# The subtractions and normalisations of the last two pairs of heads may also run on VectorE, and the order of the attention is searched anew

## The chip, the cores and the metric

The kernel runs on one core of a Trainium2 chip. The metric is device time in microseconds (us), from one launch. The kernel before was timed three times.

## What is computed

Attention over 8 batches of 8 heads (576 tokens, 64 channels), in which every score more than tau below its row's maximum is dropped, and behind it a mixture of 8 experts in which each token goes to at most one expert. Cut to what matters:

```
scores = scale * q @ k^T
keep   = scores >= max(scores) - tau
attn   = softmax over the kept scores
x      = attn @ v                                # 4608 tokens x 512
active = x @ w_skip > 0
e      = argmax(x @ w_gate);  g = its softmax weight
out    = x + active * g * (relu(x @ w1[e]) @ w2[e])
```

## The kernel before

**Tiles.** A pair of heads of one batch is one unit g; there are 32 (NG), four to a batch. Keys lie on the partitions. For each head there are four tiles of 128 keys, and a ninth tile holds the 64 remaining keys of both heads. For each pair and tile, TensorE computes scores (L797), ScalarE takes the exponential (`e`, L967), and VectorE keeps or zeroes it (`p`, L972, in float32). Two tiles of p (128 x 1152; the ninth, 128 x 576, alone) are then split in two halves of 16 bits: ScalarE or VectorE rounds p to `ph` (`fph`, by L540 or L542), and `fpl` subtracts: pl = p - ph (L1009). In `fpl` the engine is written out: `nc.gpsimd`. The product with v needs three products for each block (ph with v's high half, ph with v's low half, pl with v's high half: L1037, L1040, L1041). Before all that, the maximum of each row comes from a second computation of the scores (L824, with the maximum on VectorE at L829), and its threshold is brought into row form by transposes (L919, L923).

**Normalisation.** When both heads of a pair are done, ScalarE copies the sums out (`a`), `fz` and `fr` make the reciprocal `z`, and two multiplications write the output of the pair: `fx` (L1091, 128 x 512, tile xb) and `ft` (L1104, the 64 remaining tokens, tile x2). Both are written out as `nc.gpsimd`.

**The way to the experts.** From x come transposes (L1147), the logits (L1173, and L1234 for the remaining tokens), the gate on VectorE (L1271 to L1367), scatters of token numbers (L1395, issued on GpSimd), lists (L1638, SyncE), and gathers of rows of x for each expert (L529). The expert with most tokens is begun early: after the gate of batch 6 its number is picked, its weights are loaded and split (`wh0` on ScalarE; `wl0`, L1541, on VectorE or GpSimd), 256 of its tokens are gathered (xg0), transposed (L1570) and sent through its first layer (L1603): eight groups of 12 matmuls, which the order may put anywhere from there on. Its second layer (L1891) and the other experts follow in an order written out by hand. In it VectorE splits the second layer's weights (L1818), clears two tiles (L2029) and only then turns the lists into numbers for the next gather (L1823).

**What sets the order.** The attention's operations, up to the early first layer, are not issued in the order of the code. Each is handed to a planner (`Plan`) with a key, the operations it depends on, and a table of engines with a length for each; `place` (L210) runs forward in its own time and always takes the ready operation with the smallest rank, on the engine that is free first. An operation that names two engines is placed on either. The rank of the first pass is the key; each of the 41 numbers in SEEDS then gives a new pass, with the ranks of the pass before it shifted a little, by a number drawn from the seed. The order of the last pass is what is built. Each engine runs its own instructions strictly in that order, and waits on semaphores. Where the plan leaves TensorE without work, `emit` (L144) puts matmuls that compute nothing (`fill`, L548) in front of the next operation.

**VectorE and GpSimd.** An operation whose `port` names VectorE or GpSimd takes part in a rule of the plan: a GpSimd operation is put behind the last such VectorE operation, in the plan and with a wait in the program. p's buffers number four (PFB) and come free when `fpl` has read them; the three buffers for ph and pl (PHB) come free when TensorE has multiplied them.

Of the kernel before, what the change touches and what calls it, by code (L numbers as in the profile page):

```python
# [18 lines left out]
ALU = mybir.AluOpType  # L19
# [39 lines left out]
SHB = 2  # L59
QB = 3  # L60
EB = 2
PFB = 4
PHB = 3
HV = 4
# [25 lines left out]
)  # L90
DLAT = 0.7
OFF = dict(
    ld=-1282.9330312000948, hl=-1781.2292006134314, hlD=1248.8496803122823, loD=731.1664150661729, di=1177.335263688824, S=-1115.0015130209733, mx=-878.5280584804156, th=-441.38012807859695, tr=-924.0085545558162, tc=279.9815207656505, T=302.18323320365494, e=-632.0289199987741, p=-886.6770366002503, ph=412.4007253243831, phD=-839.1953621827544, pl=-866.5752770646977, av=358.6214955194119, ldv=-939.7929525171812, v=565.9412181202888, v0=372.25762442909286, fmA=151.44, ld0=-6.12908597837135, init=1546.1710225456764, row=-1865.5677081481308, dh=2611.857870733773, bd=-530.9955588485915, rsp=-121.81377175859078, vsp=205.19014870229796, L1=1064.7837013439314, sc=226.4129098429862,
)
# [277 lines left out]
def attn_moe_kernel(ctx: ExitStack, tc: tile.TileContext, qk, vl, tau, wg, w1, w2, out):  # L372
    nc = tc.nc
# [138 lines left out]
    NG = B * HP  # L512
    END = STEP * NG

    pl = Plan(tc)
    PE, DVE, ACT, POOL, SPQ = "PE", "DVE", "ACT", "POOL", "SP"
    BOTH = (DVE, POOL)
# [10 lines left out]
    def gather(dst, idx, n):  # L528
        return nc.gpsimd.indirect_dma_start(  # L529
            dst,  # L530
            None,
            out[0:n, :],
            bass.IndirectOffsetOnAxis(ap=idx, axis=0),
            bounds_check=n - 1,
            oob_is_err=False,
        )

    def copy(e, dst, src):
        if e == ACT:
# [4 lines left out]
    ring = pl  # L544
# [6 lines left out]
    T = {}  # L551
# [391 lines left out]
    def plan_weights(g, i):  # L943
        b, hp = divmod(g, HP)
        QK, BD = QKs[(g + 1) % QB], BDs[g % 2]
        n = STEP * g + i
        tail = i == NM
        h, kt = (2, 0) if tail else divmod(i if i < NM else i - 1, NM)
        z = ("p", g, h, kt // 2)
# [15 lines left out]
        def expo():  # L965
            T["e", g, i] = e = ap_.tile([P, 2, HS], F32, name="e", tag="e", bufs=EB)
            nc.scalar.activation(e, T["W", g, i][:, :, 0:HS], AF.Exp, bias=ntau, scale=0.125)  # L967
# [14 lines left out]
        s = pl.op(n + OFF["T"], score, deps + ring.take("sps", SPB), {PE: 1.14 if tail else 0.57})  # L982
        e = pl.op(n + OFF["e"], expo, [s] + ring.take("e", EB), {ACT: 0.66})
        m = pl.op(n + OFF["p"], mask, [s, e] + (ring.take("p", PFB) if kt % 2 == 0 else T["ms", g]), {DVE: 0.73})
        ring.free("sps", [m])
# [13 lines left out]
        nk = len(ms)  # L999
        name, bufs = ("tp", 2) if tail else ("ph", PHB)  # L1000
        w = nk * S
# [2 lines left out]
            T["ph", g, i] = ap_.tile([P, nk, S], F16, name=name + "h", tag=name + "h", bufs=bufs)  # L1004
            copy(e, T["ph", g, i], T[z][:, 0:nk])

        def fpl():
            T["pl", g, i] = ap_.tile([P, nk, S], F16, name=name + "l", tag=name + "l", bufs=bufs)
            nc.gpsimd.tensor_tensor(T["pl", g, i], T.pop(z)[:, 0:nk], T["ph", g, i], op=ALU.subtract)  # L1009

        ph = pl.op(
            n + OFF["ph"], fph, ms + ring.take(name, bufs), {ACT: w / 1200 + 0.093, DVE: w / 1920 + 0.06}, off={DVE: OFF["phD"]}, port=BOTH
        )
        lo = pl.op(n + OFF["pl"], fpl, [ph], {POOL: w * 0.00208 + 0.04})
        ring.free("p", [lo])
        T["P", g, i] = [ph, lo]
        if tail:
# [4 lines left out]
    def plan_av(g, h, parts, n):  # L1022
        b, hp = divmod(g, HP)
        hd = 2 * hp + h
        k = n + OFF["av"]
# [59 lines left out]
        zz = pl.op(k + 1, fz, [x, T["a0"]] + ring.take("z", 4), {ACT: 0.3})  # L1085
        zz = pl.op(k + 1.2, fr, [zz], {DVE: 0.11})

        def fx():
            if hp == 0:
                T["x", b] = ap_.tile([P, NM, DM], F32, name="xb", tag="xb")  # L1090
            nc.gpsimd.tensor_tensor(  # L1091
                T["x", b].rearrange("p c (h d) -> p h c d", d=D)[:, 2 * hp : 2 * hp + 2],
                T["a", g][:, :, 0:NM, 0:D],
                T["z", g][:, :, 0:NM].rearrange("p h (c o) -> p h c o", o=1).broadcast_to([P, 2, NM, D]),
                op=ALU.mult,
            )

        r0 = b % 2 * TL

        def ft():  # L1100
            if hp == 0 and b % 2 == 0:
                T["x2"] = ap_.tile([P, DM], F32, name="x2", tag="x2", bufs=1)
            rs = slice(r0, r0 + TL)
            nc.gpsimd.tensor_tensor(  # L1104
                T["x2"].rearrange("p (h d) -> p h d", d=D)[rs, 2 * hp : 2 * hp + 2],
                T["a", g][rs, :, NM, 0:D],
                T["z", g][rs, :, NM].rearrange("p (h o) -> p h o", o=1).broadcast_to([TL, 2, D]),
                op=ALU.mult,
            )

        x1 = pl.op(k + 1.5, fx, [zz] + (ring.take("xb", 2) if hp == 0 else T["xm", b, hp - 1]), {POOL: 1.1})
        xt = pl.op(
            k + 1.6, ft, [zz, x1] + (ring.take("x2", 1) if hp == 0 and b % 2 == 0 else T["xtm"][-1:]), {POOL: 0.31}
        )
        ring.free("a", [x1, xt])
        ring.free("z", [x1, xt])
# [4 lines left out]
        if hp == HP - 1 and b % 2 == 1:  # L1121
            xtm = list(T["xtm"])
# [1063 lines left out]
```

## Time and profile before

| | |
|---|---|
| device time, 3 runs | 901.28 us median (900.65 to 909.02) |
| the profiled execution, its own time | 895.38 us |
| its span | 893.5 us |
| TensorE matmul busy | 859.5 us, 96% |
| VectorE busy | 682.8 us, 76% |
| GpSimd busy | 666.6 us, 75% |
| ScalarE busy | 607.5 us, 68% |

Times in the profile's rows are microseconds from the start of the span, and lengths in microseconds, unless ns is written. PE is TensorE, DVE VectorE, ACT ScalarE, POOL GpSimd, SP SyncE (it issues most transfers). In a timeline, "[0.35 <-POOL phl L1009]" says that the engine stood idle for 0.35 us before this instruction, and that its wait was ended by GpSimd's instruction of line 1009 on tile phl. The attention ends with the last logits at 631.7 us; the experts fill the rest.

### The profile page before, as it was taken

The page shows a single profiled execution, that of the slowest core. Times are in us where ns is not written, and L with a number is a line of the kernel's source. Part 1 is how long each engine was busy: PE and PEld are TensorE (multiplying, and loading weights), DVE is VectorE, ACT ScalarE, POOL GpSimd, SP SyncE. Part 2 cuts the span into 40 slices and gives each one's busy share as a digit, 9 for nine tenths or more (in the row PEclk, how much of TensorE's full clock was granted, in tenths as well). Part 3 has the DMA queues.
Part 4 walks back from the last instruction along what each step waited for, and adds up shares of the span by engine and source line. Part 5 has one row for each costly group of instructions (what it writes and reads, how often), then busy time and mean ns, then how long its engine had stood idle before and what let it go on. Part 6 is the DMA issues. An engine that isn't in the chain of part 4 may idle for free. (4 is left out here: it accounts for less than half of the span.)

```text
span 893.5 us, 24884 instructions
## 1 busy us (share of the span) xinstructions
PE 859.5 (96%) x9745; PEld 802.5 (90%) x9745; DVE 682.8 (76%) x1605; ACT 607.5 (68%) x923; POOL 666.6 (75%) x461
## 2 busy tenths in 40 slices
PE   9999999999999999999999999989989999999997
PEld 6888999999999999998889998978879898999986
DVE  6888888988997878999888899894535554476782
ACT  1768988798988798888789878786314452454451
POOL 5576998799789798999899979999336455473463
PEclk9999999999999999999999999999999999999999
DMA  7996778569577767857865864523156635544540
GB/s 174 250 217 164 179 168 235 145 157 254 136 154 203 186 149 200 210 130 188 187 145 136 238 150 97 141 99 120 60 164 232 212 97 184 189 146 162 189 139 19
DMA packets 77422, 147.58 MB, mean 165 GB/s; under 512 B 28178, under 2 KB 28178, under 8 KB 77304
## 3 DMA queue, kind: packets, MB, share of 16 engines
q1 hardware_dynamic: 72616, 136.33, 57.9%
q0 software_dynamic: 4544, 9.65, 3.2%
q8 instruction: 77, 1.26, 0.6%
q14 instruction: 41, 0.34, 0.1%
q10 hardware_dynamic: 144, 0.00, 0.0%
HBM read 68.68 MB, written 15.21 MB: 94 GB/s over the span
## 5 line engine op out<-in xcount | busy, mean ns | idle before, releaser
L1009 POOL TENSOR_TENSOR phl<-p,phh 128x1152 f16<-128x1152 f32 x128 | 305.3, 2394 | 36.3 <-ACT phh L540 14.4
L829 DVE TENSOR_REDUCE mx<-banks 128x1 f32<-128x288 f32 x558 | 230.4, 448 | 27.6 <-PE banks L824 25.4
L972 DVE SCALAR_TENSOR_TENSOR p<-banks,e 128x576 f32<-128x576 f32 x288 | 214.3, 752 | 42.4 <-ACT e L967 38.2
L967 ACT ACTIVATE e<-banks,ntau 128x576 f32<-128x576 f32 x288 | 207.8, 739 | 49.8 <-PE banks L797 37.9
L824 PE MATMUL banks<-QK 128*128 128x288 f32 x1024 | 192.2, 306 | 6.5 <-DMA QK<-hl 4.1
L797 PE MATMUL banks<-QK 128*128 128x288 f32 x1024 | 183.6, 307 | 4.7 <-DVE p L972 2.9
L824 PEld LDWEIGHTS banks<-QK 128*128 128x128 f32 x1024 | 148.8, 188 | 11.5 <-DVE p L972 4.2
L797 PEld LDWEIGHTS banks<-QK 128*128 128x128 f32 x1024 | 145.9, 190 | 10.8 <-DVE p L972 6.3
L540 ACT ACTIVATE phh<-p 128x1152 f16<-128x1152 f32 x117 | 136.1, 1165 | 17.4 <-DVE p L972 10.8
L1037 PE MATMUL banks<-Vh,phh 128*128 128x65 f16 x1280 | 131.0, 195 | 0.4 <-ACT xf L540 0.4
L1041 PE MATMUL banks<-Vh,phl 128*128 128x65 f16 x1280 | 129.1, 194 | 1.1 <-POOL phl L1009 0.9
L1040 PE MATMUL banks<-Vl,phh 128*128 128x64 f16 x1280 | 129.9, 193 | 0.0
L1037 PEld LDWEIGHTS <-phh 128*128 128x128 f16 x1280 | 116.5, 98 | 7.1
L1041 PEld LDWEIGHTS <-phl 128*128 128x128 f16 x1280 | 117.3, 97 | 1.8 <-POOL phl L1009 1.7
L1040 PEld LDWEIGHTS <-phh 128*128 128x128 f16 x1280 | 117.5, 99 | 0.5 <-issue 0.4
L1818 POOL TENSOR_TENSOR wl<-wr,wh 128x1024 fp32r<-128x1024 f32 x28 | 72.5, 2606 | 33.5 <-ACT wh L1817 25.7
L1857 PE MATMUL hps<-xh,wl 128*128 128x256 f32 (+4 forms) x256 | 76.7, 300 | 0.0
L599 POOL TENSOR_TENSOR hl<-raw,hl 128x576 fp32r<-128x576 f32 x43 | 61.6, 1439 | 20.0 <-DVE hl L599 13.0
L1857 PE MATMUL hps<-xh,wh 128*128 128x256 f32 (+4 forms) x248 | 75.9, 306 | 0.0
L1857 PE MATMUL hps<-xl,wh 128*128 128x256 f32 (+4 forms) x248 | 74.8, 302 | 0.0
L1869 POOL DMA_INDIRECT out<-o,ids x21 | 21.1, 1004 | 71.9 <-DVE o L1868 29.2
L1858 ACT ACTIVATE QK<-hps 128x256 fp32r<-128x256 f32 (+4 forms) x64 | 26.9, 421 | 67.8 <-PE hps L1857 67.1
(251 smaller groups left out, 1882.1 us busy)
## 6 DMA issues: line engine op xcount, KB each, us to landing
QK<-hl SPq DMA_DIRECT2D x192, 288.0 KB
wr<-in_w SPq DMA_DIRECT2D x31, 1024.0 KB
raw<-in_qk SPq DMA_DIRECT2D x32, 576.0 KB
vraw<-in_vl SPq DMA_DIRECT2D x32, 320.0 KB
out<-xb SPq DMA_DIRECT2D x32, 256.0 KB
BD<-hl SPq DMA_DIRECT2D x64, 64.0 KB
QK<-QK SPq DMA_DIRECT2D x32, 76.5 KB
out<-x SPq DMA_DIRECT2D x8, 128.0 KB
```

Of the source, the lines that this page charges most:

```text
L540: nc.scalar.activation(dst, src, AF.Copy)
L797: nc.tensor.matmul(ps[:, j, 0:HS], w_, x_[:, js], start=(i == 0), stop=(i == len(mm) - 1))
L824: nc.tensor.matmul(ps[:, 0:HS], w_, x_[:, js], start=(q == 0), stop=(q == len(mm) - 1))
L829: nc.vector.tensor_reduce(T["mx", g][:, o, j : j + 1], T.pop(("S", g, i, j))[:, 0:HS], AX.X, ALU.max)
L967: nc.scalar.activation(e, T["W", g, i][:, :, 0:HS], AF.Exp, bias=ntau, scale=0.125)
L972: nc.vector.scalar_tensor_tensor(T[z][:, kt % 2].rearrange("p (a b) -> p a b", a=2), T.pop(("W", g, i))[:, :, 0:HS], 0.0, T.pop(("e", g, i ...
L1009: nc.gpsimd.tensor_tensor(T["pl", g, i], T.pop(z)[:, 0:nk], T["ph", g, i], op=ALU.subtract)
L1037: nc.tensor.matmul(pv[:, c, :], x, Vh[:, vh, kt, :], start=(j + q + c == 0), stop=False, skip_group_check=True)
L1040: nc.tensor.matmul(pv[:, c, 0:D], x, Vl[:, vh, kt, :], start=False, stop=False, skip_group_check=True)
L1041: nc.tensor.matmul(pv[:, c, :], y, Vh[:, vh, kt, :], start=False, stop=(c == NM), skip_group_check=True)
L1818: lo[q % 2].tensor_tensor(w[1][:, sl], rs, w[0][:, sl].bitcast(F32), op=ALU.subtract)
L1857: nc.tensor.matmul(hp_[:, 0:cap], w_, x, start=(i == 0), stop=(i == len(mm) - 1))
```

## The change

For the last two pairs (g = 30 and 31: `LASTS = 2`), `fpl`, `fx` and `ft` name both engines in their tables, with a length for VectorE beside that for GpSimd; for the other 30 pairs the table is as it was. 24 seeds are added behind the 41. Nothing that is computed changes, and no buffer. Line numbers of the code that follows are 9 higher in the changed kernel.

```diff
+LASTS = 2
 SEEDS = (
...
-    1038489, 1039139, 1039626, 1043379, 1053365,
+    1038489, 1039139, 1039626, 1043379, 1053365, 7000007, 7000031, 7000032, 7000052, 7000074, 7000122, 7000131,
...
+    def either(e):
+        return nc.gpsimd if e == POOL else nc.vector
+
+    def shared(g, pool, dve):
+        return {POOL: pool, DVE: dve} if g >= NG - LASTS else {POOL: pool}
...
-        def fpl():
+        def fpl(e):
             T["pl", g, i] = ap_.tile([P, nk, S], F16, name=name + "l", tag=name + "l", bufs=bufs)
-            nc.gpsimd.tensor_tensor(T["pl", g, i], T.pop(z)[:, 0:nk], T["ph", g, i], op=ALU.subtract)
+            either(e).tensor_tensor(T["pl", g, i], T.pop(z)[:, 0:nk], T["ph", g, i], op=ALU.subtract)
...
-        lo = pl.op(n + OFF["pl"], fpl, [ph], {POOL: w * 0.00208 + 0.04})
+        lo = pl.op(n + OFF["pl"], fpl, [ph], shared(g, w * 0.00208 + 0.04, w / 960 + 0.1), port=BOTH)
...
-        def fx():
+        def fx(e):
...
-            nc.gpsimd.tensor_tensor(
+            either(e).tensor_tensor(
...
-        def ft():
+        def ft(e):
...
-            nc.gpsimd.tensor_tensor(
+            either(e).tensor_tensor(
...
-        x1 = pl.op(k + 1.5, fx, [zz] + (ring.take("xb", 2) if hp == 0 else T["xm", b, hp - 1]), {POOL: 1.1})
+        x1 = pl.op(k + 1.5, fx, [zz] + (ring.take("xb", 2) if hp == 0 else T["xm", b, hp - 1]), shared(g, 1.1, 0.65), port=BOTH)
         xt = pl.op(
-            k + 1.6, ft, [zz, x1] + (ring.take("x2", 1) if hp == 0 and b % 2 == 0 else T["xtm"][-1:]), {POOL: 0.31}
+            k + 1.6, ft, [zz, x1] + (ring.take("x2", 1) if hp == 0 and b % 2 == 0 else T["xtm"][-1:]), shared(g, 0.31, 0.25), port=BOTH
         )
```

Because each pass starts from the one before, the new tables change the order from the first microseconds on: on every engine the first difference is among the first 15 planned operations. VectorE gets six of the ten subtractions of the two pairs (pair 30: three of its four wide ones; pair 31: three of its four wide ones), and both pairs' fx and ft.

GpSimd at the end of the attention, before, from the last scatters for batch 6 to the last subtraction (numbers tell tiles apart; phl and tpl are pl of a wide and of a ninth tile):

```order
L1395 DMA lst_68<-rec_11134,si_11136 36864x2 x3
L1009 TENSOR_TENSOR tpl_11728<-p_11561,tph_11598 128x576
L1009 TENSOR_TENSOR phl_11745<-p_11609,phh_11706 128x1152
L1009 TENSOR_TENSOR phl_11781<-p_11726,phh_11765 128x1152
L529 DMA xg0_11841<-out_0,id0_149 128x512 x2
L1009 TENSOR_TENSOR phl_11903<-p_11763,phh_11822 128x1152
L1009 TENSOR_TENSOR tpl_11930<-p_11901,tph_11912 128x576
L1009 TENSOR_TENSOR phl_11966<-p_11820,phh_11920 128x1152
L1009 TENSOR_TENSOR phl_11985<-p_11914,phh_11971 128x1152
L1009 TENSOR_TENSOR phl_12063<-p_11969,phh_12029 128x1152
L1091 TENSOR_TENSOR xb_11429<-a_11418,z_11730 128x2x4x64
```

The same place after the change, from the last scatters for batch 6 to the scatters for the last gate:

```order
L1404 DMA lst_68<-rec_11235,si_11237 36864x2 x4
L1100 TENSOR_TENSOR xb_11283<-a_11445,z_11616 128x2x4x64
L1018 TENSOR_TENSOR tpl_11936<-p_11903,tph_11919 128x576
L1113 TENSOR_TENSOR x2_10074<-a_11445,z_11616 64x128
L1018 TENSOR_TENSOR phl_12001<-p_11934,phh_11977 128x1152
L532 DMA xg0_12016<-out_0,id0_149 128x512 x2
L1550 TENSOR_TENSOR wl0_12091<-wr_11829,wh0_11932 128x512
L1404 DMA lst_68<-rec_12227,si_12229 36864x2 x5
```

Eight subtractions stood behind these scatters, and now two; the gather xg0 stood before the last five subtractions, and now stands behind the last.

VectorE around the last p of pair 31, after the change (id0 are the numbers for the gather xg0, wl0 the early weights' low halves; before, only p's, two reciprocals, id0 and wl0 stood there):

```order
L981 SCALAR_TENSOR_TENSOR p_11999<-banks_104,e_11970 128x576
L1507 CAST id0_149<-rec0_148 128x2
L1508 TENSOR_SCALAR id0_149<-rec0_148 128x2
L981 SCALAR_TENSOR_TENSOR p_11999<-banks_104,e_11995 128x576
L1196 TENSOR_TENSOR lg_10977<-lg_10977,banks_104 128x64
L1100 TENSOR_TENSOR xb_11283<-a_11757,z_11853 128x2x4x64
L1018 TENSOR_TENSOR phl_12064<-p_11999,phh_12013 128x1152
L1550 TENSOR_TENSOR wl0_12091<-wr_11829,wh0_11932 128x512
L1550 TENSOR_TENSOR wl0_12125<-raw2_11851,wh0_11932 128x512 x2
L1550 TENSOR_TENSOR wl0_12091<-wr_11829,wh0_11932 128x512
L1092 RECIPROCAL z_12136<-z_12136 128x10
```

The last subtraction and the normalisation of pair 30 have come into VectorE's queue, and four of the wl0 subtractions stand between that subtraction and the last reciprocal.

TensorE around the last logits, before: the third of the early first layer's groups of 12 ends here, and three such groups stand ahead of the last logits (L1234, L1173) and five behind:

```order
L1603 MATMUL banks<-QK_105,wl_11714 128x256
L1147 MATMUL banks<-ident,xb 128x128 x4
L1173 MATMUL banks<-wgt,xf 128x16 x6
L1147 MATMUL banks<-ident,x_10097 128x128 x4
L1173 MATMUL banks<-wgt,xf 128x16 x2
L1147 MATMUL banks<-ident,xb 128x128 x4
L1234 MATMUL banks<-wgt,xf 128x16 x4
L1173 MATMUL banks<-wgt,xf 128x16 x4
L1603 MATMUL banks<-QK_105,wh_11532 128x256
```

The same place after the change (L557 is `fill`, L1579 the transposes of the gathered tokens):

```order
L1579 MATMUL banks<-ident,xg_12016 128x128 x8
L557 LDWEIGHTS jt
L557 MATMUL banks<-jt 128x256
...
L1156 MATMUL banks<-ident,x_10074 128x128 x4
L1156 MATMUL banks<-ident,xb 128x128 x4
...
L1243 MATMUL banks<-wgt,xf 128x16 x4
L1182 MATMUL banks<-wgt,xf 128x16 x4
L1612 MATMUL banks<-QK_105,wh_11932 128x256
```

All eight groups of 12 now stand behind the last logits. Of the matmuls that compute nothing, 27 stood in the attention's last part before, and now 30; in its first 40 us there were 87, and now there are 95.

## Rows read from the trace of the kernel before

**Rows 1.** Busy time by stretch: engine, busy time, instruction count, then clock, transfers.

```profile
75.00:575.00 500.00, 486.93 (x6741) 464.47 (x6738) 433.90 (x1117) 422.60 (x631) 445.19 (x280) 1.00 0.70 173
...
575.00:600.00 25.00, 23.61 (x329) 21.12 (x328) 23.82 (x64) 21.10 (x32) 23.52 (x16) 1.00 0.26 94
600.00:625.00 25.00, 21.90 (x341) 20.27 (x340) 13.81 (x23) 16.42 (x26) 23.57 (x16) 0.93 0.31 110
```

**Rows 2.** Groups by line: GpSimd's wide subtraction; busy, mean ns, idle before.

```profile
L1009 POOL TENSOR_TENSOR phl<-p,phh 128x1152 f16<-128x1152 f32 x128 | 305.3, 2394 | 36.3 <-ACT phh L540 14.4
```

**Rows 3.** Timeline of GpSimd at the end of the attention: start, length, instruction.

```profile
614.72 7.04 POOL L1009 TENSOR_TENSOR phl<-p,phh 128x1152 f16<-128x1152 f32 x3
...
625.92 1.05 POOL L1091 TENSOR_TENSOR xb<-a,z 128x512 f32<-128x512 f32 x1 [1.08 <-DVE z L1083]
```

**Rows 4.** Timeline of TensorE, 595 to 617 us: its longer waits.

```profile
597.75 0.20 PE L1041 MATMUL banks<-Vh,phl 128*128 128x65 f16 x1 [0.35 <-POOL phl L1009]
...
599.37 0.78 PE L797 MATMUL banks<-QK 128*128 128x288 f32 x4 [0.59 <-ACT QK L929]
...
601.99 0.79 PE L797 MATMUL banks<-QK 128*128 128x288 f32 x4 [1.16 <-DVE p L972]
...
603.57 0.20 PE L1041 MATMUL banks<-Vh,tpl 128*128 128x65 f16 x1 [0.71 <-POOL tpl L1009]
...
615.85 0.99 PE L1570 MATMUL banks<-ident,xg 128*128 128x128 f32 x7 [1.10 <-DMA xg<-out,id]
```

**Rows 5.** Timeline of TensorE: matmuls that compute nothing, and eight score matmuls twice.

```profile
600.00 0.83 PE L548 MATMUL banks<-jt 128*128 128x256 f16 x6
...
604.23 2.27 PE L797 MATMUL banks<-QK 128*128 128x288 f32 x8
...
611.22 1.30 PE L797 MATMUL banks<-QK 128*128 128x288 f32 x8
```

**Rows 6.** Early first layer (L1603) by stretch: matmul busy, weight loads, granted clock.

```profile
631.50:637.20 5.70, 5.66 (x36) 5.62 (x37) 0.75 0.04 12
637.30:640.30 3.00, 2.98 (x25) 2.78 (x24) 1.00 0.00 0
```

**Rows 7.** Timeline of TensorE: last scores, last product, last logits, next expert's transposes.

```profile
612.50 0.77 PE L797 MATMUL banks<-QK 128*128 128x288 f32 x4
...
623.52 0.20 PE L1037 MATMUL banks<-Vh,phh 128*128 128x65 f16 x1
...
624.45 0.63 PE L1147 MATMUL banks<-ident,xb 128*128 128x128 f32 x4
...
630.37 1.33 PE L1173 MATMUL banks<-wgt,xf 128*128 128x16 f32 x8
...
655.17 1.45 PE L1839 MATMUL xtp<-ident,xg 128*128 128x128 f32 x4 [2.85 <-DMA xg<-out,ids]
```

**Rows 8.** Timeline of VectorE: last p, and its queue ahead of the next gather.

```profile
616.18 0.76 DVE L972 SCALAR_TENSOR_TENSOR p<-banks,e 128x576 f32<-128x576 f32 x1 [1.22 <-ACT e L967]
...
641.89 4.63 DVE L1818 TENSOR_TENSOR wl<-wr,wh 128x1024 fp32r<-128x1024 f32 x4 [0.25 <-ACT wh L1817]
...
648.40 1.34 DVE L2029 MEMSET xg<- 128x1536 f32 x1 [0.27 <-issue]
650.45 0.17 DVE L1823 CAST ids<-recs 128x2 int32<-128x2 f32 x1 [0.71 <-DMA recs<-lst]
```

**Rows 9.** Subtractions on VectorE by line: shortest, median, longest ns, starts, shape.

```profile
L1541 DVE TENSOR_TENSOR wl<-wr,wh x4: 678/678/2090, 596.2 to 599.4; 128x512 fp32r<-128x512 f32 x4
...
L1818 DVE TENSOR_TENSOR wl<-wr,wh x32: 1202/1225/7786, 641.9 to 874.0; 128x1024 fp32r<-128x1024 f32 x32
```

**Rows 10.** Timeline of GpSimd: the subtraction that ran at 596 us.

```profile
595.31 2.39 POOL L1009 TENSOR_TENSOR phl<-p,phh 128x1152 f16<-128x1152 f32 x1
```

**Rows 11.** Timelines: ScalarE's last ph, and GpSimd's second early gather.

```profile
617.70 1.16 ACT L540 ACTIVATE phh<-p 128x1152 f16<-128x1152 f32 x1
...
610.09 1.01 POOL L529 DMA_INDIRECT xg<-out,id  x1 [0.31 <-PE banks L797]
```

2 rows, old and new, of the table SEEDS are left out of this document.

## The prediction

> **What bounds the kernel now.** I read the busy times by stretch first, then the timelines of GpSimd, TensorE and VectorE at the end of the attention, then the durations by line. Between 75 and 575 us TensorE is busy 486.93 of 500 us, and nothing else comes near it [rows 1]: what counts there is TensorE's own 13.1 us of idle time. The picture changes behind 575 us. GpSimd is busy 23.52 and 23.57 of 25 us in the next two stretches, while TensorE falls to 21.90 in the second and its mean granted clock to 0.93 [rows 1]. The reader should see a backlog: GpSimd is still at three wide subtractions from 614.72 to 621.76 [rows 3], although the last p of the attention was done at 616.94 [rows 8], and the last product with v starts only at 623.52 [rows 7].
>
> What TensorE loses here can be summed up to 640.3 us, where the early first layer ends [rows 6]. Waits: 0.35 + 0.59 + 1.16 + 0.71 + 1.10 = 3.9 us [rows 4]. The 27 matmuls that compute nothing: six take 0.83 us, 0.14 each [rows 5], so 3.7 us. Slow clock: the eight score matmuls at 604.23 take 2.27 us, the same eight at 611.22 only 1.30 [rows 5], 1.0 us lost; and behind the logits 36 matmuls take 5.66 us at a granted clock of 0.75, where 25 take 2.98 at 1.00 (0.119 each, so 36 would take 4.3) [rows 6], 1.4 us; a mean of 0.75 is a mix of the clock's two levels, 1.2 and 2.4 GHz, and what TensorE did just before were the logits' small matmuls. Together 10.0 us, 1.1% of the time. That is all that the last part could give if TensorE's work stays as it is.
>
> Behind 640.3 another chain takes over. VectorE splits weights (4.63 us from 641.89), clears two tiles (the second ends at 649.74) and makes the numbers for the next expert's gather at 650.45, after 0.71 us of waiting for the lists [rows 8]; TensorE waits 2.85 us for that gather until 655.17 [rows 7]. So two things nearly tie there: the last logits (631.70 [rows 7]) plus 23.5 us, by gate, scatters and lists, and the end of the early first layer plus 14.9 us, by VectorE's queue; without the 0.71 us, 14.2.
>
> **The change, step by step.** *Off GpSimd:* six wide subtractions of 2.394 us [rows 2], 14.4 us, and two pairs' normalisations, 1.05 us for each fx [rows 3]. *Onto VectorE:* the same subtraction has not run there. Two inputs in SBUF of 512 columns take 0.678 us, of 1024 columns 1.202 to 1.225 [rows 9]; the slope gives 1.34 us for 1152. The upper bound is 1.34 plus a whole GpSimd subtraction, 3.73 us, if it stands behind one; I take 1.34, since in the new order GpSimd has only two subtractions left behind the scatters. Six make 8.0 us. fx lies between 0.68 (same width, rows 9) and GpSimd's 1.05; I take 0.68. ft is smaller and bounded by it. VectorE had 11.2 us idle between 600 and 625 [rows 1], so this fits, but not with much room.
>
> *Up to the last scores.* Before, the last score matmul ends at 613.27 [rows 7]. The waits before it are the first four, 2.8 us, with 16 of the 27 empty matmuls (2.2) and the slow 1.0: 6.0 us that the backlog costs there. In the new order 6 empty matmuls stand before it (0.8), and I leave 2.0 us of waits, since VectorE is now nearly full; the ends are 0 and 4 (as much as all five waits of rows 4). But 60 product matmuls and a group of transposes now come ahead of it, which stood behind: 30 products take the 0.93 us from 623.52 to the next transposes, and those 0.63 [rows 7], so 2.5 us. So the last scores end at 613.3 - 6.0 + 0.8 + 2.0 + 2.5 = 612.6.
>
> *From the last scores to the last logits.* Before, 18.4 us: 3.7 to the end of the last p [rows 7, 8], 4.8 until GpSimd's last subtraction, 1.8 until TensorE, busy with a group of the early layer, turns to the product, 8.2 to the end of the logits, another group of 12 among them (1.4 at 0.119). After: 3.7, then 1.16 for ph [rows 11] and 1.34 for pl, then 8.2 - 1.4 = 6.8 for the rest. I add 1.0: the gather xg0 now stands behind GpSimd's last subtraction, its transposes stand ahead of the last transposes of x in TensorE's queue, and its second half took 5.8 us from issue to use [rows 4, 11]. Sum 14.0, so the last logits end at 626.6, 5.1 us earlier.
>
> *And behind them* this is taken back in part. Three groups of the early first layer have left the space before the logits, and all eight now follow: 96 matmuls at 0.119 [rows 6] are 11.4 us, and the early layer ends at 638.0 instead of 640.3, only 2.3 earlier. VectorE's queue then needs its 14.2 us, so the next expert's transposes start at 652.2; by the logits alone they could start at 650.1. Before, 655.17: **3.0 us gained**, not 5.1. The second half of the weights for the second layer is now loaded behind the output rows, but stays covered by those 11.4 us. *First microseconds:* eight more empty matmuls, 0.14 each, **1.1 us lost**. *Between 75 and 575 us* the order is new everywhere; the 13.1 us of idle may be less or more. Bounds: 0 (a stretch like the best) and twice as much, 26 us, as the 575 to 600 stretch lost 1.39 in 25 us [rows 1], a rate of 28 in 500. I take no change.
>
> Sum: -3.0 + 1.1 = -1.9 us. The profiled execution's own time of 895.38 (its span and 1.9 us around it) would become 893.5; it lies 5.9 us under the median of the three runs, 901.28, and from that median the sum gives **899.4 us**.
>
> **The port.** Where VectorE subtracts while GpSimd is inside a subtraction, the two do not share: GpSimd's ran from 595.31 to 597.70 at its usual 2.39 [rows 10], while the first of VectorE's four, begun at 596.2, is the one of 2.09 instead of 0.678 [rows 9], which is about the wait to 597.70 and 0.6 more. The Trainium skill, page "SBUF — State Buffer", section "Who interferes with whom", states this as a rule: a VectorE instruction with two inputs in SBUF and a GpSimd instruction that reads SBUF exclude each other, and whoever comes second blocks fully. This row agrees with it. It speaks against the change, which puts exactly such instructions into VectorE's queue, ahead of p.
>
> **Rivals.** *The whole backlog comes out.* GpSimd's queue really is short now, and if VectorE hides all it gets, the early layer ends earlier by all 10.0 us, VectorE's queue follows without its 0.7 of waiting, and with 1.1 lost at the start the time is 891.7. Against it: 30 empty matmuls still stand in the order, so TensorE's gaps are expected to stay; it decides if TensorE's waits up to 640 us come to under 1 us.
>
> *The change does not do what it says.* The gaps are only moved from GpSimd to the chain p, product, normalisation, logits: 30 empty matmuls cost 4.2 us, waits and slow clock stay at 6.3, the early layer ends 0.5 later, VectorE's queue gains its 0.7, and with 1.1 at the start the time is 902.2.
>
> *VectorE is blocked by GpSimd* (the port, above), and p waits behind it. Place: from the first moved subtraction to the last p. GpSimd's reading instructions left there are a wide and two narrow subtractions, an fx and an ft, at most 2.39 + 2 x 1.20 + 2 x 1.05 = 6.9 us (a narrow one taken as half a wide one, ft as an fx). If VectorE stood behind all of it, p and the early layer come 6.9 later: 906.3, slower than before. It decides if over 2 us of the moved subtractions' time is above 1.34 each. For it: rows 10. Against it: the plan keeps them apart, and scatters, which are no reading of tiles that long, fill GpSimd there.
>
> *The new order of the middle decides.* 13 us of idle there, halved or half as much again, gives 892.9 or 905.9; doubled, 912.5. Nothing in the profile of before favours a sign.
>
> **How the numbers follow.** My forecast has 0.50 (its own range 896 to 904, from the waits of 0 to 4 us and the clock's 2.4), the whole backlog 0.15, no effect 0.13, blocked VectorE 0.07, the middle 0.15, half to each side. About 1%, 9 us, is what a measurement of this kernel can tell from no change. Below 892.3 lie somewhat over half of the whole-backlog case (0.09), half of the better middle (0.04), and a tail of the forecast (0.05): 0.18. Above 910.3 lie the worse part of the middle (0.04) and tails of the others (0.04): 0.08. The rest, 0.74, is within 1%. The range 890 to 907 leaves out about a tenth on each side.
>
> **What would show it.** Right: VectorE's six wide subtractions at 1.3 to 1.4 us; GpSimd idle before its last subtraction; the last logits some 5 us earlier than 631.7, counted against the middle's shift; the early layer's end only about 2 us earlier; the numbers for the next gather then no longer waiting for the lists, but for VectorE's tile clears; TensorE waiting longer than 2.85 us for that gather. Wrong: VectorE subtractions of 2 us and more; the early layer's end moving as far as the logits; a gap of several us before the gathered tokens' transposes; or TensorE's idle between 75 and 575 us far from 13.1.

## The result, and the profile after

| | median | lowest to highest | ratio to before |
|---|---|---|---|
| before, 15 runs | 902.42 us | 900.45 to 909.02 | |
| changed, 15 runs | 905.91 us | 900.09 to 912.41 | 1.0066 [1.0042, 1.0090] |

The changed kernel is slower: by 0.7% by the ratio, by 0.4% by the two medians (the ratio is not formed from them). Its interval leaves out 1. Forecast were 899.4 us. The time lies inside the range of 890 to 907 and inside 1% of before, but on the other side of it.

Busy time by stretch, changed kernel (columns as in [rows 1], from TensorE to GpSimd, then the granted clock, the share of transfers and GB/s):

```profile
0.00:75.00 75.00, 71.86 (x717) 61.31 (x718) 59.82 (x155) 43.37 (x62) 48.48 (x72) 1.00 0.81 197
75.00:575.00 500.00, 482.82 (x6625) 462.05 (x6621) 426.12 (x1082) 415.55 (x621) 437.31 (x274) 0.99 0.70 173
575.00:600.00 25.00, 22.48 (x276) 21.32 (x276) 17.94 (x63) 17.03 (x25) 17.47 (x14) 0.93 0.15 52
600.00:625.00 25.00, 22.46 (x397) 20.87 (x396) 22.68 (x47) 19.87 (x32) 17.58 (x16) 1.00 0.27 89
```

GpSimd's backlog is gone: 17.47 and 17.58 us busy of 25 where [rows 1] has 23.52 and 23.57. But between 75 and 575 us TensorE now stands idle 17.2 us instead of 13.1, and its clock there is no longer full.

Timelines of the changed kernel at the end of the attention (start, length, instruction, in brackets the idle time before it and who ended it): first VectorE's share of the moved work, then TensorE's last scores and last logits, as in [rows 7]:

```profile
615.65 1.36 DVE L1018 TENSOR_TENSOR phl<-p,phh 128x1152 f16<-128x1152 f32 x1 [1.43 <-ACT phh L549]
620.46 1.35 DVE L1018 TENSOR_TENSOR phl<-p,phh 128x1152 f16<-128x1152 f32 x1
627.91 0.68 DVE L1100 TENSOR_TENSOR xb<-a,z 128x512 f32<-128x512 f32 x1
...
622.72 0.77 PE L806 MATMUL banks<-QK 128*128 128x288 f32 x4
636.91 1.04 PE L1182 MATMUL banks<-wgt,xf 128*128 128x16 f32 x8
```

And the way to the next expert, on VectorE, GpSimd, SyncE (SPq) and TensorE; it answers to [rows 7, 8]:

```profile
651.17 4.63 DVE L1827 TENSOR_TENSOR wl<-wr,wh 128x1024 fp32r<-128x1024 f32 x4 [0.31 <-issue]
656.08 1.34 DVE L2038 MEMSET xg<- 128x1536 f32 x1 [0.27 <-issue]
657.69 1.34 DVE L2038 MEMSET xg<- 128x1536 f32 x1 [0.27 <-issue]
658.94 0.11 DVE L1832 CAST ids<-recs 128x2 int32<-128x2 f32 x1
...
659.94 1.05 POOL L532 DMA_INDIRECT xg<-out,ids  x1 [8.06 <-issue]
661.29 1.01 POOL L532 DMA_INDIRECT xg<-out,ids  x1 [0.30 <-issue]
...
653.00 6.67 SPq L1647 DMA_DIRECT2D recs<-lst  x8
659.92 1.03 SPq L528 DMA_DIRECT2D wr<-in_w  x2
...
666.85 0.45 PE L1848 MATMUL xtp<-ident,xg 128*128 128x128 f32 x1 [5.31 <-DMA xg<-out,ids]
667.81 0.90 PE L1848 MATMUL xtp<-ident,xg 128*128 128x128 f32 x3 [0.51 <-DMA xg<-out,ids]
```

The reader should see two things. The numbers for the gather (ids) stand directly behind the second tile clear and no longer wait for the lists, as forecast. And the gather now leaves at 659.94 and 661.29, just when SyncE, done with the eight list reads, issues two weight loads of 1 MB each for the third expert (659.92). TensorE waits for its first half until 666.85 and for its second until 667.81, 5.6 and 6.5 us after the second issue. Before, the same gather left ahead of those loads, and the first half was there 2.3 us after the second issue ([rows 7]: 655.17; that row merges the transposes of both halves, and the second half's begins at 655.72, 2.9 us after the issue):

```profile
652.86 1.01 POOL L529 DMA_INDIRECT xg<-out,ids  x1 [0.31 <-issue]
...
655.79 1.03 SPq L525 DMA_DIRECT2D wr<-in_w  x2
```

In a second trace of before (experiment 1) the two halves stand apart, 2.4 and 3.1 us after the second issue:

```profile
651.26 1.01 POOL L530 DMA_INDIRECT xg<-out,ids  x1 [0.30 <-issue]
...
653.66 0.45 PE L1840 MATMUL xtp<-ident,xg 128*128 128x128 f32 x1 [2.67 <-DMA xg<-out,ids]
654.31 0.90 PE L1840 MATMUL xtp<-ident,xg 128*128 128x128 f32 x3 [0.20 <-DMA xg<-out,ids]
```

Where TensorE's clock went in the middle, changed kernel, by 5 us (same columns as above), and the waits ahead of it:

```profile
215.00:220.00 5.00, 3.29 (x28) 3.06 (x26) 1.68 (x5) 2.08 (x3) 2.22 (x1) 1.00 0.91 299
220.00:225.00 5.00, 4.38 (x22) 4.38 (x22) 4.29 (x10) 3.25 (x6) 3.06 (x3) 0.62 0.81 189
225.00:230.00 5.00, 5.00 (x29) 4.85 (x29) 3.72 (x10) 0.00 (x0) 0.00 (x0) 0.50 0.57 164
230.00:235.00 5.00, 5.00 (x110) 4.92 (x108) 3.52 (x18) 2.63 (x5) 2.35 (x1) 0.86 0.02 3
360.00:365.00 5.00, 4.45 (x79) 4.37 (x80) 3.02 (x10) 4.24 (x8) 4.09 (x3) 0.66 0.80 235
...
220.62 0.66 PE L806 MATMUL banks<-QK 128*128 128x288 f32 x3 [2.33 <-DVE p L981]
360.56 0.53 PE L806 MATMUL banks<-QK 128*128 128x288 f32 x2 [2.75 <-ACT a L549]
```

Time times (1 - granted clock) is taken here as what a slow clock costs, an estimate that takes TensorE as busy throughout: 1.9 + 2.5 + 0.7 behind the wait at 220 us, 1.7 behind the one at 360, 6.8 us together. In the trace of before no stretch of 5 us between 75 and 575 us is under full clock, and the longest wait there is 1.27 us.

So two theories stood. **T:** the move does its work, but the late end turns it into a new wait (the gather that meets the loads). **M:** the new seeds and tables have set a new order for the whole attention, and this order waits longer in the middle, which also costs clock.

### The profile page after: what moved, and what is told of

It is laid out like the page before. It is cut to its first block, busy times and chain, and to the rows that moved or that the text cites. A ratio compares the mean times of both kernels' runs of the same rounds, so it can differ in the third digit from the quotient of the medians.

```text
span 906.9 us, 24874 instructions
## 1 busy us (share of the span) xinstructions
PE 864.1 (95%) x9755; PEld 808.2 (89%) x9755; DVE 690.7 (76%) x1612; ACT 606.9 (67%) x923; POOL 650.5 (72%) x454
## 3 DMA queue, kind: packets, MB, share of 16 engines
q8 instruction: 78, 1.28, 0.6%
## 5 line engine op out<-in xcount | busy, mean ns | idle before, releaser
L1018 POOL TENSOR_TENSOR phl<-p,phh 128x1152 f16<-128x1152 f32 x122 | 291.5, 2398 | 41.5 <-PE banks L806 9.3
L833 PE MATMUL banks<-QK 128*128 128x288 f32 x1024 | 191.3, 309 | 3.8 <-DVE p L981 1.9
L806 PE MATMUL banks<-QK 128*128 128x288 f32 x1024 | 180.1, 307 | 9.8 <-DVE p L981 5.3
L549 ACT ACTIVATE phh<-p 128x1152 f16<-128x1152 f32 x114 | 132.2, 1163 | 30.6 <-PE banks L1050 13.5
L1827 POOL TENSOR_TENSOR wl<-wr,wh 128x1024 fp32r<-128x1024 f32 x28 | 72.4, 2603 | 35.0 <-ACT wh L1826 19.9
L608 POOL TENSOR_TENSOR hl<-raw,hl 128x576 fp32r<-128x576 f32 x45 | 64.3, 1437 | 24.6 <-DVE hl L608 12.4
```

The lines of the kernel that those rows point to most:

```text
L549: nc.scalar.activation(dst, src, AF.Copy)
L806: nc.tensor.matmul(ps[:, j, 0:HS], w_, x_[:, js], start=(i == 0), stop=(i == len(mm) - 1))
L833: nc.tensor.matmul(ps[:, 0:HS], w_, x_[:, js], start=(q == 0), stop=(q == len(mm) - 1))
L1018: either(e).tensor_tensor(T["pl", g, i], T.pop(z)[:, 0:nk], T["ph", g, i], op=ALU.subtract)
L1827: lo[q % 2].tensor_tensor(w[1][:, sl], rs, w[0][:, sl].bitcast(F32), op=ALU.subtract)
```

## The experiments

Every ratio is to runs of the kernel before on the same chip.

**1 and 2. Both kernels once more**, without an edit.

> The kernel before once more, against itself, for a second trace. Its first profiled execution took 895.38 us, less than each of its 15 timed runs (900.45 to 909.02). If that trace is a lucky execution, a second one shows what a common one has: TensorE's granted clock falling at some wait between 75 and 575 us, where the first trace shows 1.00 throughout, and a span near 900. If the first trace is a common one, the clock stays at 1.00 there and the span is again near 894. Ratio 1.000 either way.

> The changed kernel once more, for a second trace. Its first trace shows two waits of 2.33 us (at 220.6) and 2.75 us (at 360.6) with the clock down to 0.50 to 0.86 behind them, about 7 us of lost clock between 75 and 575 us. Theory M (the new order of the middle costs): the same two waits stand in this trace too, at the same instructions, and the clock falls behind at least one; ratio 1.004 to 1.009. Theory T (only the end costs): the middle's waits differ and cost little, and the 5.3 us wait for the next expert's gather is there; ratio the same.

Before: 897.71 against 898.60 us, 1.0011 [0.9987, 1.0034], span 893.7. Changed: 902.76 us, 1.0053 [1.0033, 1.0073], span 898.9. Both profiled executions of before (895.38 and 895.48 us) took less than the median of their runs (902.42 and 897.71), so both its traces show a good execution. Of the changed kernel's two waits in the middle one stands again (1.73 us at 220.4, clock 0.80 and 0.86 behind it), and the other does not. The difference stands, and these two traces show how much of it is fixed. From the end of the early first layer to the next expert's transposes it is 14.9 and 14.7 us in the two traces of before, 17.3 and 17.4 in the two of the changed kernel: fixed. The middle is not: 17.2 us of idle time and 6.8 us of lost clock in the changed kernel's first trace, 14.7 and 1.7 in its second; before has 13.1 and 13.2, and no lost clock.

**3 and 4. The move without the new order, and the new order without the move.** An operation of the two pairs is held on GpSimd in all passes but the last (3, with the 41 old seeds), or in the last pass alone (4, with the 65; this edit is shown):

```diff
+        kept = [["POOL"] if o.only else x for o, x in zip(ops, self.opts)]
         for n, s in enumerate(seeds):
             p = self.step(s, span)
+            if n == len(seeds) - 1:
+                self.opts = kept
```

> The order of the kernel before (41 seeds), and only its last pass may put the last two pairs' subtractions and normalisations on VectorE: on every engine the order is that of before up to about 610 us; two subtractions (one narrow, one wide) and one pair's normalisation move. Theory M: no loss, 0.996 to 1.000 of before, since the middle is before's; at the end up to 2 us gained. Theory T or blocked VectorE: the moved work makes the end later, 1.003 or more.

> The order of the changed kernel (65 seeds), but its last pass puts all ten subtractions and both normalisations of the last two pairs on GpSimd as before: the order is that of the changed kernel up to about 600 us. Theory M: as slow as the changed kernel or slower, 1.005 to 1.014, since it keeps the middle and gives back what the move gained at the end (3 to 6 us). Theory T (the move itself costs): back to 1.000 to 1.003.

Move alone: 897.18 us, 0.9987 [0.9965, 1.0009]; only two subtractions and one pair's products left GpSimd, and the middle stays as it was (14.5 us of idle time, no lost clock). In this trace VectorE is blocked by GpSimd, as one of the prediction's rivals had it: its narrow subtraction (tpl), begun inside one of GpSimd's, takes 2.34 us and its wide one 1.80, where experiment 10's narrow one takes 0.75 and the changed kernel's wide ones 1.35.

```profile
613.54 2.41 POOL L1020 TENSOR_TENSOR phl<-p,phh 128x1152 f16<-128x1152 f32 x1
...
614.23 2.34 DVE L1020 TENSOR_TENSOR tpl<-p,tph 128x576 f16<-128x576 f32 x1
```

New order alone: 914.03 us, 1.0185 [1.0151, 1.0219], slower than theory M's range. In this order the move is worth 1.2 to 1.3% of the time. The gather meets the loads here too: these go out at 668.72, the gather's second half at 670.37, and TensorE waits 6.23 us for it. So the late end comes with the order and not with the move. But the 1.2 to 1.3% are not a price of the move by itself: with the backlog back on GpSimd, the plan put 101 matmuls that compute nothing behind 575 us, where the changed kernel has 30, 71 more at 0.14 us each, 9.9 us. Beside them stand 13.7 us of idle time and 6.9 of lost clock in the middle, and 17.3 and 6.8 between 575 and 700 us, where before has 9.1 and 5.1 and the changed kernel 14.8 and 5.1.

**5. The tile clears off VectorE's queue** (T's wait made shorter). In the changed kernel:

```diff
     for x in xgs:
-        nc.vector.memset(x, 0.0)
+        nc.gpsimd.memset(x, 0.0)
```

> The changed kernel with one edit: the two tile clears ahead of the next expert's gather go to GpSimd, which is idle there, so that VectorE's numbers for the gather (ids) come up to 3.1 us earlier. Theory G (the late gather meets the 2 MB of weights that the third expert needs, which are issued behind the lists, and is slowed by them): the gather is out before those loads, its second half lands about 2.3 us after its issue and not 5.6, TensorE's wait at the transposes falls from 5.3 to about 0 to 2 us and the early layer's end plus 17.3 us becomes plus 11 to 13; 5 to 6 us gained, ratio to before 0.998 to 1.001. Rival S (the gather takes 5.6 us of its own there, VectorE's queue is merely late): the start moves by the 3.1 us of the clears alone, ratio 1.001 to 1.004. Rival M (only the middle costs): nothing gained, 1.005 to 1.007.

898.03 us, 0.9966 [0.9929, 1.0002]. More is gained than forecast. (The 2.3 and 5.6 us in this and the next two expectations are the first half's; the second half's are 2.9 and 6.5.) TensorE does not wait for the gather any more, and the second issue is out before the loads. From the early layer's end to the transposes it is 13.8 us, where 11 to 13 were expected, since TensorE has other work until then:

```profile
644.65 2.74 POOL L2038 MEMSET xg<- 128x1536 f32 x2
649.89 1.05 POOL L532 DMA_INDIRECT xg<-out,ids  x1 [2.50 <-issue]
651.25 1.01 POOL L532 DMA_INDIRECT xg<-out,ids  x1 [0.31 <-issue]
...
652.72 22.08 SPq L528 DMA_DIRECT2D wr<-in_w  x5
...
656.05 0.60 PE L1848 MATMUL xtp<-ident,xg 128*128 128x128 f32 x4
```

A part of the gain is clock: behind its wait of 5.3 us the changed kernel has a granted clock of 0.50 and 0.82 from 665 to 675 us, 3.4 us lost; here 1.7 are lost from 645 to 650 us (0.66), and nothing from 650 to 675.

**6. The loads held behind the gather** (T's collision taken away, nothing made earlier): a dependency of the third expert's first weight load on the gather issued last at that place of the program.

```diff
+                tc.add_manual_dep(
+                    loads[0],
+                    reads[-1].ins.name,
+                    mybir.DependencyInfo(mybir.DependencyClass.Sync, mybir.DependencyReason.DATA),
```

> The changed kernel with one edit: the third expert's first weight loads wait until the next expert's gather has landed. Nothing becomes earlier on VectorE. Theory G: the second half of the gather lands 2.0 to 2.8 us after its issue instead of 5.6, TensorE's wait at the transposes falls from 5.3 to about 2 us, 3 us gained, ratio to before 1.001 to 1.004 if the loads, now some 3 us later, are still covered. Rival S: the gather still takes over 5 us, ratio 1.005 to 1.007 or worse.

901.97 us, 1.0005 [0.9972, 1.0039]. The gather issued last is not this one but the one after it (three parts, from 667.67 to 671.33), so the loads are held longer than the expectation says: SyncE waits 16.8 us for it behind the list reads, and not some 3. No harm is seen from it: from the transposes to the end TensorE stands idle 7.8 us, in the two traces of the changed kernel 8.3 and 8.8. The gather in question, issued just as late by VectorE's queue, is alone, and its halves are there 2.2 and 2.7 us after the second issue, instead of 5.6 and 6.5:

```profile
658.52 1.01 POOL L532 DMA_INDIRECT xg<-out,ids  x1 [0.30 <-issue]
...
660.73 0.30 PE L1848 MATMUL xtp<-ident,xg 128*128 128x128 f32 x1 [1.93 <-DMA xg<-out,ids]
661.24 0.75 PE L1848 MATMUL xtp<-ident,xg 128*128 128x128 f32 x3 [0.20 <-issue]
...
673.94 13.44 SPq L528 DMA_DIRECT2D wr<-in_w  x6
```

**7. The collision put into the kernel before**, by clearing both tiles twice on VectorE:

```diff
         nc.vector.memset(x, 0.0)
+        nc.vector.memset(x, 0.0)
```

> The kernel before with one edit: VectorE clears the two tiles twice, so that the numbers for the next expert's gather come 3.2 us later, and with them the gather, which now goes out when the third expert's weight loads do. Theory G: more is lost than the 3.2 us: the gather's second half lands 4.5 to 5.6 us after its issue instead of 2.3, TensorE waits 8 to 9.5 us at the transposes instead of 2.85, ratio 1.0055 to 1.0075. Rival S: TensorE waits 6.0 us, ratio 1.003 to 1.004.

907.06 us, 1.0076 [1.0047, 1.0106]. For 3.2 us of clears, TensorE waits 8.9 us instead of 2.85; the loads go out 0.3 us after the gather's second issue, and the second half needs 6.2 us from there:

```profile
656.07 1.01 POOL L529 DMA_INDIRECT xg<-out,ids  x1 [0.30 <-issue]
...
656.38 1.03 SPq L525 DMA_DIRECT2D wr<-in_w  x2
...
658.40 0.45 PE L1839 MATMUL xtp<-ident,xg 128*128 128x128 f32 x1 [5.47 <-DMA xg<-out,ids]
662.31 0.90 PE L1839 MATMUL xtp<-ident,xg 128*128 128x128 f32 x3 [3.46 <-DMA xg<-out,ids]
```

**8. The same clears on GpSimd in the kernel before** (control for 5; the edit is the same).

> The kernel before with the two tile clears on GpSimd instead of VectorE. It is the control for the same edit in the changed kernel, which brought 0.3% below before. Theory G (the gather was hurt only because VectorE's queue had become late and let the weight loads come first): before, the numbers for the gather already wait for the lists and not for the clears, so nothing is gained: TensorE's wait at the transposes stays at 2.5 to 2.9 us, ratio 0.998 to 1.001. Rival (the clears on VectorE cost some 3 us in any version, and the edit alone explains the gain of the changed kernel): the wait falls to about 0, ratio 0.994 to 0.997.

897.02 us, 0.9996 [0.9968, 1.0024]: nothing gained. Its numbers wait 3.85 us for the lists and TensorE 3.22 us for the gather (2.5 to 2.9 expected). The clears cost only where VectorE's queue has become the later of the two. With 5 to 8, T's collision is shown from both sides.

**9 and 10. Two other orders:** the new seeds without the option (`LASTS = 0`), and the option with only the 41 old seeds (the 24 numbers deleted).

> The changed kernel with no pair that may choose (LASTS = 0): the 24 new seeds alone, with the old tables. Theory M (any new order of the middle moves TensorE's waits by several us, and waits over 2 us cost clock behind them): TensorE's idle time plus lost clock between 75 and 575 us comes out several us off the 13.1 of before, to either side; by the changed kernel's example 18 to 24, ratio 1.005 to 1.02 with the backlog at the end back. Rival E (only the end counts): the middle is within 2 us of 13.1 and the ratio 0.998 to 1.003.

> The changed kernel with the old 41 seeds alone: the same subtractions may be VectorE's from the first pass on, the 24 new seeds are left out. Theory M (what an order costs in the middle and in empty matmuls is set anew by every search, and the option does not help of itself): this order holds 172 matmuls that compute nothing where before has 115 and the changed kernel 125, 57 more at 0.14 us each, 8 us; with waits between 75 and 575 us of 13 to 18 us the ratio is 1.004 to 1.015. Rival T (the option itself brings the gain at the end, whichever order is around it): faster than before by up to 0.5%, ratio 0.995 to 1.000.

909.46 us, 1.0093 [1.0066, 1.0120], and 916.14 us, 1.0188 [1.0150, 1.0227]. The first is as M says in time but not in place: 14.8 us of idle time and 1.7 of lost clock in the middle, together 16.5, lie between E's bound (15.1) and M's 18. The rest is lost at the end, with 40 empty matmuls behind 575 us (before 27) and the backlog back on GpSimd (21.28 and 21.61 us busy of 25 from 575 to 625 us). The second is slower than M's range: its middle has 17.5 us of idle and 3.4 of lost clock, with the 57 more empty matmuls of 8 us. That the option brings a gain in any order is refuted; an order found anew can cost 1 to 2% with or without it.

**11 and 12. One exchange in the middle.** The wait at 220 us has a plain cause in ScalarE's queue in the changed kernel: a copy (hl) waits 3.15 us for TensorE, and the exponential behind it is what p, and the score matmuls, need:

```profile
217.92 1.16 ACT L549 ACTIVATE hl<-raw 128x1152 fp32r<-128x1152 f32 x1 [3.15 <-PE banks L833]
218.99 0.72 ACT L976 ACTIVATE e<-banks,ntau 128x576 f32<-128x576 f32 x1
```

The edit puts this one copy two places later in ScalarE's queue, once in the changed kernel and once on top of experiment 5; no other engine's order moves:

```diff
+        if emit:
+            act = [o for o in out if o.on == "ACT"]
+            n = next(i for i, o in enumerate(act) if o.fn.__name__ == "hi" and 214 < o.t0 < 215)
+            out.remove(act[n])
+            out.insert(out.index(act[n + 2]) + 1, act[n])
```

> The changed kernel with two places exchanged in ScalarE's queue and nothing else: a copy of an input's high half (line 549, tile hl, at 217.9 us in its trace), which waits there 3.15 us for TensorE, goes behind the exponential and the copy xf that stood behind it. Theory M (the new order's long waits in the middle cost themselves and a fallen clock behind them): TensorE's 1.7 to 2.3 us of waiting for p at about 220 us, present in all four executions of this order, is gone, the granted clock at 220 to 235 us stays at 1.00, 4 to 5 us gained in the mean, ratio to before 1.000 to 1.002. Rival W (the wait only moves: the copy is late now, and its subtractions, transfers and score matmuls after it): idle time between 75 and 575 us stays at 14 to 17 us, ratio 1.004 to 1.007.

> The same exchange on top of the two clears on GpSimd. If M holds and the tail and the middle add up, the ratio to before is 0.990 to 0.994, below both kernels; with rival W it stays at 0.995 to 0.999.

903.11 us, 1.0025 [0.9995, 1.0054], and **895.65 us, 0.9939 [0.9910, 0.9969]**, faster than both kernels. The wait at 220 us is gone and the clock stays full there (the second of the two, where the exponential now runs at 214.65):

```profile
214.65 0.74 ACT L981 ACTIVATE e<-banks,ntau 128x576 f32<-128x576 f32 x1
...
215.00:220.00 5.00, 4.95 (x42) 4.72 (x40) 4.70 (x12) 3.84 (x6) 2.71 (x3) 1.00 0.79 265
220.00:225.00 5.00, 5.00 (x64) 4.92 (x64) 4.57 (x15) 1.78 (x3) 2.52 (x2) 1.00 0.92 210
```

By the ratios the exchange is worth 0.28% without experiment 5's edit (1.0025 beside 1.0053), or 0.41% (beside 1.0066), and 0.27% with it (0.9939 beside 0.9966): 2.4 to 3.7 us of the 4 to 5 expected. These ratios lie on different chips and their intervals overlap, and 1.0025 is between M's range and rival W's, so what the exchange alone is worth stays open. W's idle time of 14 to 17 us is met by the first (14.8 us, and 3.4 of lost clock); the second has 13.7 and 5.1. Together that is 18.2 and 18.8 us, where the four traces of the changed kernel's order have 19.9 in the mean. The wait at about 355 us stays (2.74 and 3.22 us), with 3.4 us of lost clock from near its end on. What is shown is that both edits together bring this order below before.

## Why the prediction was wrong, step by step

**Right: the move itself.** VectorE's subtraction was estimated at 1.34 us and takes 1.35 to 1.36; fx at 0.68 takes 0.68 to 0.69. The blocked VectorE, a rival with 7%, did not come in this order, where the plan keeps the two apart: the excess over 1.34 is some hundredths of a microsecond where over 2 us was its condition. Experiment 3 shows that it comes in another.

**Right in its place, not in its gain: the end up to the early first layer.** Counted against the shift that the kernel has by 575 us. In the first trace of the changed kernel that shift is -1.5 us of idle time up to 75 us, +4.1 of idle time and +6.8 of clock in the middle, and 7 more empty matmuls (95 before 575 us, 88 in before) at 0.14 (1.0), 10.4 us; in the second -0.3 + 1.6 + 1.7 + 1.0 = 4.0.

| | forecast | first trace, less its shift | second, less its shift |
|---|---|---|---|
| last scores end | 612.6 | 613.1 | 611.6 |
| from there to the last logits | 14.0 | 14.5 | 14.2 |
| logits to the early layer's end | 11.4 | 11.6 | 11.6 |
| early layer's end | 638.0 | 639.1 | 637.3 |

But the 640.3 us of before, from which the forecast counts, is one trace's. Before's other traces (1, 7, 8), less their own shifts, end the early layer at 638.0, 638.9 and 638.2, the changed kernel's other two (5, 6) at 637.5 and 639.1. In the mean of four and four the end comes 0.6 us earlier and not 2.3 (the last logits 4.1, forecast 5.1). The slow clock that the prediction booked as the backlog's cost (1.0 + 1.4 us) was that trace's: from 575 us to the early layer's end it lost 3.4 us of clock, the others 0 to 1.7. And TensorE's idle time from 575 us, shift counted, to the last scores did not fall, 3.5 to 4.0 us where before has 2.9 to 4.4; that the place came out as forecast is partly luck.

**Wrong: "VectorE's queue then needs its 14.2 us".** This is the step that failed: measured were 17.3 and 17.4. The 14.2 were before's 14.9 less the wait for the lists, and held the gather's landing as it was. I named the numbers, the clears and a longer TensorE wait, but not what else starts when the gather does. The list reads take SyncE 6.7 to 6.9 us, and behind them stand the loads; before, the gather was ahead of them by 2.9 us. In the prediction's sum, "3.0 us gained" becomes 640.3 - 638.0 less 2.5, nothing gained (-0.2). Behind the longer wait 3.4 us of clock are lost, in both traces; before lost 1.7 in its first trace (0.67 from 655 to 660 us) and 3.4 in its second. The Trainium skill, page "DMA: Bandwidth & Descriptors", section "Queues, rings and completion order", says that each DMA engine takes turns, packet by packet, between the queues that have work for it. The traces are in line with it, though they do not show the turns: the last half is there 2.7 to 3.1 us after its issue alone, and after 6.2 to 7.1 beside two loads.

**Wrong: "I take no change" between 75 and 575 us.** Each of the two orders has four traces there. Before's (the traces before and of experiments 1, 7, 8): idle 13.1, 13.2, 14.1, 12.5 us, lost clock 0, 0, 1.7, 1.7. The changed kernel's (after, 2, 5, 6): idle 17.2, 14.7, 15.0, 15.8, lost clock 6.8, 1.7, 3.4, 5.2. In the mean 2.5 us of idle and 3.4 of clock: 5.9 us lost. Both together are 14.1 us before and 19.9 after in the mean; experiment 4, whose order is the changed kernel's up to about 600 us, has 20.6, and the orders of 9 and 10 have 16.5 and 20.9. This cost is read from traces. The one run that took a wait of the middle away by itself (11) brought no gain clear of the noise. The rival of the middle had this sign at half of its 15%, but it was priced by idle time alone, and the clock behind the waits is the larger part.

**The sum again.** Start, -1.2 (idle, mean of the same traces) + 1.0 (empty matmuls), -0.2; middle 5.9; up to the early layer's end -0.6; from there to the transposes 2.6; behind them 0.9 (238.4 and 240.0 us to the end before, 240.0 and 240.2 after, two traces each). That is 8.6 us slower by the traces. The ratios say 4.8 to 6.0 (0.53 and 0.66%), the medians 3.5 to 4.2. The traces overstate it: before's four profiled executions lie 3.9 us below the medians of their runs in the mean, the changed kernel's four 0.6, and these 3.3 us off the sum leave 5.3.

The mean granted clock that is on record with each timed run gives a second count. Span times (1 - clock) is 7.3 us in the mean of 27 runs of before and 11.1 us in the 10 of the changed kernel beside them (experiment 2): 3.8 of the 4.1 us between their means. By this estimate what the move gains and what the new waits lose cancel on that chip, and the clock behind the waits is what is left. For experiment 11 this count gives 11.7 us (before there 8.0), for 12 8.1, for 5 9.4 (before there 7.9): the clock that the exchange was to give back is not seen in 11.

With the meeting of gather and loads taken away (5 and 6) the changed kernel is no longer slower than before, and with it put into before (7) before is slower by 0.8%, of which the later clears alone were expected to make 0.3 to 0.4. So this meeting is shown as the cause that turned the forecast round. That the middle cost a part as well is argued from the traces above.

**What stays open.** The wait at 352 to 360 us: 2.67 to 3.22 us in five of the six traces of this order, ended by ScalarE's copy `a`. Before that copy ScalarE itself stood idle, 3.24 us in the changed kernel's trace, for something that the trace gives only as remote. It was not tried, and neither was an order that has both this end and before's middle.

## What to carry to other kernels

When a change moves work off a queue at one place, ask what the next queue starts at its new time, and what other transfers stand at that time; a gather of a few rows was cheap here only as long as it was ahead of the big loads. A search whose seeds or tables change is a change of the whole kernel: price its middle with waits and the clock behind them, or keep the old order up to the place that you want to change and look what is left of the gain. Where a chain ends in two things that nearly tie, shorten the second before the first. And take more than one trace of before: a fall of the clock in one is not yet a cost of the kernel.

## What was not expected of the hardware

**What a wait costs TensorE beyond itself.** Ten traces have the order of before or that of the changed kernel between 75 and 575 us (but for the one exchange). All eight waits of 2.2 us and more in them have, from near their end on, stretches of a lower granted clock, 0.50 to 0.90 over 5 us, a mix of 1.2 and 2.4 GHz, which cost 1.7 to 5.1 us each. Of six waits of 1.70 to 1.95 us two have such a stretch behind them, at 1.7 us each, and of three of 1.5 to 1.6 us none. Two more falls of 1.7 us stand behind waits of only 0.83 and 1.28 us, so the wait's length is not all that decides. The eight long waits come to 21.0 us and the clock with them to 22.2, so a wait of over 2 us cost here about twice itself.

**What loads cost a gather.** The two halves of a gather of 256 rows are there 2.2 to 2.8 us (the first) and 2.7 to 3.1 us (the second) after the second issue when they are alone. Beside two loads of 1 MB, issued from 1.4 us before it to 0.3 us after, the last half takes 6.2 us (experiment 7) to 7.1 (experiment 2). The transfers then run at 411 GB/s (664 to 668 us in the changed kernel), where before's gather had 99:

```profile
664.00:668.00 4.00, 0.64 (x2) 0.38 (x3) 0.00 (x0) 0.00 (x0) 0.00 (x0) 0.62 1.03 411
...
652.00:656.00 4.00, 1.05 (x5) 0.47 (x4) 0.00 (x0) 0.00 (x0) 2.59 (x3) 0.86 0.43 99
```
